# Weight sums in a two-layer attention and gated-MLP kernel, ordered behind the attention's last residual addition

## The chip, the cores and the metric

The kernel runs on one core of one Trainium2 chip. The metric is device time in microseconds (us), the median of several executions. The engines are named as the profile names them: PE does matmuls, DVE, ACT and POOL do elementwise work, SP issues most of the DMAs. ACT issues some as well. Each engine takes its own instructions in a fixed order, and semaphores hold an instruction until what it needs is done.

## The reference

Two layers, applied twice with the same weights, on x of 2048 tokens by 1024 features:

```python
x = x + A(layernorm(x))     # attention without softmax, 32 heads of 32
x = x + B(layernorm(x))     # gated MLP, 3584 hidden features
x = x + A(layernorm(x))
x = x + B(layernorm(x))
# A: q, k, v = x @ wqkv; phi(t) = where(t > 0, t + 1, exp(t)) + 1e-6
#    kv = phi(k)^T v; z = sum of phi(k); o = phi(q) kv / (phi(q) z + 1e-6); return o @ wo
# B: h = relu(x @ W_gate) * (x @ W_up); return h @ W_down
```

## The kernel before

Tokens come in 16 tiles of 128 (`x[t]`, resident in fp32). The four layers run one after the other: `layer_A(0)`, `layer_B(1)`, `layer_A(2)`, `layer_B(3)`.

**End of the attention.** `out_unit` makes one half (512 columns) of one token tile: eight matmuls (L557) into one PSUM bank, then the residual addition on DVE (L564) into `x[t]`. There are four such banks (tag "a"), so PE can run four units ahead of DVE. The first quarter of the tiles is done first, then quarters 1, 2 and 3. Beside them DVE and POOL still scale later quarters (L511 to L523), and the layer norm of the next layer already runs on finished tiles: statistics on DVE (L154, L159), `rstd` and the scaled tile `xnb` on ACT (L161, L162, L188), a transposing DMA issued on SP (L347) into `xnT`, and then the token sums `sums_x` on DVE (L712 to L715).

**The gated layer.** `layer_B` takes the tokens in two halves (`c`). Each 2x2 block product is done with seven products instead of eight (a Strassen-Winograd scheme), which needs sums of token blocks (`sums_x`) and sums of weight blocks. A unit `u` (`glu`, 14 per half) has two hidden tiles; for gate ("g") and up ("u") it makes seven products of four matmuls each (L739). Products 1, 2 and 3 read the raw weights, products 4 to 7 the sums. On the way DVE adds partial results (`zg`, `zu` at L770, `m5g`, `m5u` at L773), ACT copies and applies relu (L747, L756, L760), and DVE or POOL multiplies gate by up (L750, L777).

**The weight sums.** They are the same for all four passes over the weights, so they are formed once, during the first half of the first gated layer, and stored to DRAM; the later passes load them. `make_gu` forms the three sums of one gate or up weight tile on DVE, one instruction of 128x1024 elements (L677) and two of 128x512 (L679, L680), and stores them with a DMA on ACT's queue (L681). `make_d` loads two units' down weights into the tile `wd` (L690, on SP), forms four sums of 128x1024 elements (L694 to L697) and stores them (L698).

**What sets the order.** A list of later tasks (`_Later`) holds steps with a delay in ticks; a tick is one unit of the running stage, or one product of `glu`. The sums of unit 0 are entered at the start of the attention's last quarter with delay 1, those of unit u+1 at the start of unit u with delay 4, those of `make_d` with delay 4. The order of emission is only a priority: except inside `manual_schedule` blocks, a scheduler orders each engine's instructions by its own estimate of when their inputs are ready, and it may put a sum that is emitted late ahead of an addition that is emitted early. The weight loads go through a ring (`_Ring`) of slots in a pool of 16 buffers, issued on SP in program order; a load waits until its buffer's last reader is done and until an earlier DMA on the same semaphore has landed.

Of the kernel before, what the change touches and what calls it, by code (L numbers as in the profile page):

```python
# [8 lines left out]
ALU = mybir.AluOpType  # L9
# [80 lines left out]
class _Net:  # L90
# [313 lines left out]
    def layer_A(self, l, last_ln):  # L404
        nc, G, KT, D = self.nc, self.G, self.KT, self.D
        ring, later = self.ring, self.later
# [53 lines left out]
        def m_units(d):  # L460
            mt = self.temp([P, D], BF16, name=f"mt{l}_{d}")
            for h in range(H):
                ps = self.ps3.tile([P, NW], F32, tag="b")
                for t in range(self.ST):
                    nc.tensor.matmul(ps, lhsT=self.xn[l, t][:, d * P:(d + 1) * P],  # L465
                                     rhs=self.pk[l, t][:, h * NW:(h + 1) * NW],
                                     start=(t == 0), stop=(t == self.ST - 1))
                    if t == self.ST // 2 - 1:
                        later.tick()
                nc.scalar.activation(out=mt[:, h * NW:(h + 1) * NW], in_=ps, func=ACT.Copy)  # L470
                if h == H - 1:
                    later.at(2, lambda: kv_step(d, mt))
                later.tick()
# [30 lines left out]
        def z_chain(i):  # L504
            z_mult(*divmod(i, QT))
            if i < 10:
                later.at(2, lambda: z_chain(i + 1))

        def z_mult(sc, j):
            prod = ksum  # L510
            nc.gpsimd.tensor_tensor(out=prod, in0=pq_of[sc, j], in1=zrow, op=ALU.mult)  # L511
            later.at(2, lambda: z_sum(prod, sc, j))
# [17 lines left out]
        def fold_wo(n):  # L530

            n2, a = divmod(n, H)
            if n2 == 0:
                T.append(self.slot(f"T{l}_{a}", [P, 4, D]))
            ps = [pool.tile([P, NW], F32, tag=tag, name=f"fold{l}_{n}_{i}") for i, (pool, tag) in
                  enumerate(((self.kvp, "kv0"), (self.kvp, "kv1"), (self.ps3, "b"), (self.ps3, "b")))]
            wo = ring.get((l, f"o{n2}"))
            for b in range(R):
                g = a * R + b
                for i in range(R):  # L540
                    e = slice(i * HD, (i + 1) * HD)
                    nc.tensor.matmul(ps[i][b * HD:(b + 1) * HD, :], lhsT=kvT[e, g, e],
                                     rhs=wo[e, g, :], start=True, stop=True,
                                     tile_position=(i * HD, b * HD))
            for i in range(R):
                g = a * R + i
                dst = T[g // 4][:, g % 4, n2 * NW:(n2 + 1) * NW]
                if g % 2:
                    nc.scalar.activation(out=dst, in_=ps[i], func=ACT.Copy)
                else:  # L550
                    nc.vector.tensor_copy(out=dst, in_=ps[i])

        def out_unit(sc, j, n2):
            t = sc * QT + j
            ps = self.ps.tile([P, NW], F32, tag="a")
            for g in range(G):
                nc.tensor.matmul(ps, lhsT=pqT[sc][:, g, j * P:(j + 1) * P],  # L557
                                 rhs=T[g // 4][:, g % 4, n2 * NW:(n2 + 1) * NW],
                                 start=(g == 0), stop=(g == G - 1))
            cols = slice(n2 * NW, (n2 + 1) * NW)  # L560
            xs = self.x[t][:, cols]


            nc.vector.tensor_tensor(out=xs, in0=self.xb[t][:, cols] if l == 0 else xs,  # L564
                                    in1=ps, op=ALU.add)


        def column_major(f, q):
            return [lambda j=j, c=c: f(q, j, c) for c in range(H) for j in range(QT)]

        def row_major(f, q):
            return [lambda j=j, c=c: f(q, j, c) for j in range(QT) for c in range(H)]

        def run(*lists):

            n = max(len(u) for u in lists)
            for i in range(n):
                for u in lists:
                    if i < len(u):
                        u[i]()  # L580
                        later.tick()
# [26 lines left out]
        with self.tc.manual_schedule(engines={mybir.EngineType.DVE, mybir.EngineType.Pool}):  # L608
            ring.free_before((l, "v0"))
            later.at(5, z_row)  # L610
            later.at(7, lambda: z_chain(0))
            for d in range(KT):
                m_units(d)
            if l > 0:
                later.at(1, lambda: [self.bring_back(t) for t in range(self.NS)])
            q3 = row_major(q_unit, self.NQ - 1)
            out0 = column_major(out_unit, 0)

            def with_fold(u, i):
                return lambda: (u(), fold_wo(i // 2) if i % 2 == 0 else None)  # L620

            run(q3[:2])
            run([with_fold(u, i) for i, u in enumerate(q3[2:] + out0[:1])])
            run(out0[1:3])
            ring.free_slowly((l, "o0"), later, 2)
            for i in range(11, self.ST):
                later.at(1 + 3 * (i - 11), lambda i=i: z_mult(*divmod(i, QT)))
            run(out0[3:])
            for sc in range(1, self.NQ):
                if sc < 3:  # L630
                    self.ln_later(last_ln, sc - 1, 0, 3, 2)
                if sc == 2:
                    for j in range(QT):
                        later.at(3 * j + 6, lambda j=j: self.sums_x(last_ln, 0, j))
                if sc == 3 and l == 0:
                    for w in "gu":
                        later.at(1, lambda w=w: self.make_gu(ring.get((last_ln, 0, w, 0)), w, 0))
                run(row_major(out_unit, sc))


# [43 lines left out]
    def make_d(self, u):  # L684

        v = self.nc.vector
        t = self.slot(f"wd{u}", [P, 2, 4, NW])
        T = t[:, :, :, :].bitcast(F16)
        us = slice(u, u + 2)
        self.nc.sync.dma_start(out=t[:, :, :, :].rearrange("p u (h n) f -> p u h (n f)", h=2),  # L690
                               in_=self.wd_v[:, :, us, :].rearrange("p h u n -> p u h n"))

        def sums():
            v.tensor_tensor(out=T[:, :, 0, :], in0=t[:, :, 1, :], in1=t[:, :, 0, :], op=ALU.subtract)  # L694
            v.tensor_tensor(out=T[:, :, 1, :], in0=t[:, :, 3, :], in1=t[:, :, 1, :], op=ALU.subtract)
            v.tensor_tensor(out=T[:, :, 3, :], in0=t[:, :, 3, :], in1=T[:, :, 0, :], op=ALU.subtract)
            v.tensor_tensor(out=T[:, :, 2, :], in0=t[:, :, 2, :], in1=T[:, :, 3, :], op=ALU.subtract)  # L697
            self.later.at(1, lambda: self.nc.scalar.dma_start(  # L698
                out=self.td[:, us, :, :], in_=T))

        self.later.at(4, sums)

    def sums_x(self, l, c, j):

# [151 lines left out]

    def layer_B(self, l, final):
        ring = self.ring
        for c in range(2):
            hT = []  # L860
            first = l == 1 and c == 0
            for u in range(self.U):
                if u % 2 == 0:
                    hT.append(self.slot(f"h{l}_{c}_{u // 2}", dtype=F16))
                ring.load_to(ring.index((l, c, "g", u)) + 5)
                if first:
                    if u + 1 < self.U:
                        self.later.at(4, lambda u=u: [self.make_gu(ring.get((l, c, w, u + 1)), w, u + 1)
                                                      for w in "gu"])
                if first and u % 2 == 0:  # L870
                    self.make_d(u)
                self.glu(l, c, u, hT)
                if c == 0 and u == (self.U - 1 if first else 0):
                    after = self.last_put.ins
            if c == 0:
                self.ln_chunk(l, 1, 20, 3, 3, after)
            elif not final:
                self.ln_later(l + 1, 0, 28, 6, 4)
            self.down(l, c, hT, final)
# [68 lines left out]
```

## Time and profile before

| | us |
|---|---|
| median of 7 runs | 1500.2 |
| range of the 7 runs | 1498.98 to 1506.29 |
| the profiled execution | 1506.29 |
| its span in the trace | 1504.5 |
| PE busy | 1481.6 |
| DVE busy | 824.2 |
| ACT busy | 508.9 |
| POOL busy | 274.0 |

The profiled execution is the slowest of the seven. A line of the profile names an operation by its source line, the engine, and the tiles that it writes and reads; "ps<-T,pqT" is the attention's output product, "x<-x,ps" the residual addition, "w<-w" a sum of gate or up weights, "wd<-wd" a sum of down weights. Times are us from the start of the span unless marked ns. A bracket behind a row of the timeline is the time that its engine idled before it, and what ended that. The times of one stretch can be held against those of another that does the same work: the first and the second attention, or the two passes over the first token half.

### The profile page before, as it was taken

Reading aid. Unit: us, or ns where it says so; the run is one execution under the profiler, and the core shown is the slowest. Engines: PE = TensorE matmul, PEld = TensorE weight load, DVE = VectorE, ACT = ScalarE, POOL = GpSimd, SP = SyncE. Lnnn points to the kernel's source line nnn. Section 1 sums busy time; section 2 is a strip of 40 time slices with the busy share of each in tenths; the row PEclk is TensorE's granted clock in tenths of the full one; section 3 lists DMA queues with packets and bytes.
Section 4 is the critical chain, followed back from the end, with each engine's and each line's share of the span. In section 5 each row is a group of like instructions: output and inputs, shape, how many; then the busy total and the mean of one; then the engine's idle time right before and its main releaser. Section 6 shows DMA issues by size and latency. Waiting matters only on the chain.

```text
span 1504.5 us, 18590 instructions
## 1 busy us (share of the span) xinstructions
PE 1481.6 (98%) x7039; PEld 671.8 (45%) x7039; DVE 824.2 (55%) x1427; ACT 508.9 (34%) x911; POOL 274.0 (18%) x190
## 2 busy tenths in 40 slices
PE   9999998998899999999999999999999999999999
PEld 4444443443344444444444444444444444444444
DVE  8855588665585533447256645875335433444632
ACT  6751322333341243332047523233333203333300
POOL 1349340111000011110013474401111000111000
PEclk9999999999999999999999999999999999999999
DMA  9502449774568974435923027494344689444461
GB/s 276 102 29 49 113 79 292 252 228 171 185 199 204 318 242 139 140 129 169 269 42 71 29 43 227 90 285 140 113 150 137 195 239 293 140 140 140 147 210 42
DMA packets 313754, 242.92 MB, mean 161 GB/s; under 512 B 105280, under 2 KB 290880, under 8 KB 312768
## 3 DMA queue, kind: packets, MB, share of 16 engines
q1 hardware_dynamic: 302688, 214.07, 49.3%
q10 hardware_dynamic: 10976, 27.66, 4.9%
q8 instruction: 55, 0.90, 0.3%
q14 instruction: 35, 0.29, 0.1%
HBM read 186.65 MB, written 30.41 MB: 144 GB/s over the span
## 4 chain that ended last, share of the span: by engine, by line
PE 90%; DMA 4%; DVE 4%; issue 1%; ACT 0%; SPq 0%; DVEq 0%
PE ps L430 15%; PE dy L822 10%; PE yu L739 9%; PE yg L739 9%; PE ps L465 7%; PE dv L822 6%; PE dx L822 6%; PE xu L739 6%; PE xg L739 6%; PE zu L739 3%; PE zg L739 3%; PE vu L739 3%; PE vg L739 3%; PE ps L557 3%; DMA wd<-in_B_W_down_dram 3%; DVE x L564 1%
## 5 line engine op out<-in xcount | busy, mean ns | idle before, releaser
L739 PEld LDWEIGHTS <-w 128*128 128x128 f16 (+1 forms) x3136 | 307.3, 98 | 384.0 <-issue 15.2
L777 POOL TENSOR_TENSOR h<-m5u,m5g 128x512 f16<-128x512 f32 x56 | 72.0, 1286 | 832.9 <-DVE m5u L773 808.7
L430 PE MATMUL ps<-w,xnT 128*128 128x512 bf16 x1024 | 223.4, 379 | 0.2 <-ACT xnT L291 0.2
L822 PEld LDWEIGHTS <-h 128*128 128x128 f16 x1120 | 109.6, 98 | 132.2
L770 DVE TENSOR_TENSOR zg<-yg,m5g 128x512 f32<-128x512 f32 x56 | 39.1, 699 | 208.6 <-PE yg L739 204.4
L430 PEld LDWEIGHTS <-xnT 128*128 128x128 bf16 x1024 | 99.4, 98 | 119.9 <-issue 1.4
L739 PE MATMUL yu<-s,w 128*128 128x512 f16 x448 | 115.8, 381 | 6.9 <-DVE zu L770 6.8
L557 PE MATMUL ps<-T,pqT 128*128 128x512 bf16 x512 | 113.9, 385 | 6.6 <-DVE x L564 6.6
L739 PE MATMUL yg<-s,w 128*128 128x512 f16 x448 | 115.0, 379 | 3.3 <-DVE zg L770 3.3
L739 PE MATMUL xu<-xnT,w 128*128 128x512 f16 x448 | 115.1, 379 | 0.0
L739 PE MATMUL xg<-xnT,w 128*128 128x512 f16 x448 | 115.0, 379 | 0.0
L747 ACT ACTIVATE m5g<-m5g 128x512 f32<-128x512 f32 x56 | 35.2, 629 | 189.4 <-DVE m5g L773 183.9
L822 PE MATMUL dy<-w,h 128*128 128x512 f16 x448 | 98.0, 379 | 0.0
L822 PE MATMUL dx<-w,h 128*128 128x512 bf16 x448 | 97.3, 379 | 0.0
L511 POOL TENSOR_TENSOR kvc<-pq,kvc 128x1024 f32<-128x1024 bf16 x32 | 68.0, 2124 | 84.5 <-DVE den L516 71.1
L557 PEld LDWEIGHTS <-pqT 128*128 128x128 bf16 x512 | 50.5, 99 | 69.2 <-issue 10.9
L154 DVE BATCH_NORM_STATS2 stats<-x 128x6 f32<-128x512 f32 (+1 forms) x120 | 76.4, 672 | 0.5 <-DMA x<-in_A_x_dram 0.2
L161 ACT ACTIVATE rstd<-mv,eps 128x1 f32<-128x1 f32 x64 | 18.0, 289 | 156.0 <-DVE mv L159 155.8
L380 DVE SCALAR_TENSOR_TENSOR pq<-ps,e 128x512 bf16<-128x512 f32 x64 | 44.0, 687 | 48.5 <-ACT e L374 46.8
L516 DVE TENSOR_REDUCE den<-kvc 128x32 f32<-128x1024 f32 x32 | 38.9, 1215 | 54.1 <-POOL kvc L511 54.1
L447 POOL TENSOR_TENSOR kvc<-kvc,slab 128x512 f32<-128x512 f32 x46 | 53.9, 1179 | 78.2 <-DVE slab L380 60.9
L822 PEld LDWEIGHTS <-e 128*128 128x128 f16 x448 | 43.9, 98 | 52.8
(105 smaller groups left out, 1924.8 us busy)
## 6 DMA issues: line engine op xcount, KB each, us to landing
w<-in_B_W_gate_dram SPq DMA_DIRECT2D x56, 512.0 KB, 6.1
w<-in_B_W_up_dram SPq DMA_DIRECT2D x56, 512.0 KB, 4.6
w<-td SPq DMA_DIRECT2D x32, 896.0 KB, 4.7
w<-in_B_W_down_dram SPq DMA_DIRECT2D x24, 896.0 KB, 5.2
w<-tg SPq DMA_DIRECT2D x42, 512.0 KB, 6.9
w<-tu SPq DMA_DIRECT2D x42, 512.0 KB, 5.9
w<-in_A_wqkv_dram SPq DMA_DIRECT2D x10, 1024.0 KB, 8.5
tg<-w ACTq DMA_DIRECT2D x14, 512.0 KB, 5.2
```

The costliest lines, as they stand in the source:

```text
L154: self.nc.vector.bn_stats(out=stats[:, c, :], in_=src[:, c * fmax:(c + 1) * fmax])
L380: nc.vector.scalar_tensor_tensor(out=out, in0=ps, scalar=0.0, in1=e, op0=ALU.max, op1=ALU.add)
L430: nc.tensor.matmul(by_row(ps), lhsT=self.xnT[l, l_q][:, kt, j * P:(j + 1) * P], rhs=w[:, kt, :].rearrange("p (b i d) -> p i b d", i=R, d=H ...
L447: nc.gpsimd.tensor_tensor(out=ksum[:, cols], in0=ksum[:, cols], in1=pk, op=ALU.add)
L465: nc.tensor.matmul(ps, lhsT=self.xn[l, t][:, d * P:(d + 1) * P], rhs=self.pk[l, t][:, h * NW:(h + 1) * NW], start=(t == 0), stop=(t == sel ...
L511: nc.gpsimd.tensor_tensor(out=prod, in0=pq_of[sc, j], in1=zrow, op=ALU.mult)
L516: nc.vector.tensor_reduce(out=den, in_=heads(prod), axis=mybir.AxisListType.X, op=ALU.add)
L557: nc.tensor.matmul(ps, lhsT=pqT[sc][:, g, j * P:(j + 1) * P], rhs=T[g // 4][:, g % 4, n2 * NW:(n2 + 1) * NW], start=(g == 0), stop=(g == G ...
L739: nc.tensor.matmul(ps, lhsT=W[w][m][:, k, :], rhs=A[m][:, k, :], start=start and k == 0, stop=k == 3, skip_group_check=True)
L770: nc.vector.tensor_tensor(out=Z[w], in0=Y[w], in1=V[w], op=ALU.add)
L777: nc.gpsimd.tensor_tensor(out=h[:, 3, :], in0=V["u"], in1=V["g"], op=ALU.mult)
L822: nc.tensor.matmul(banks[j], lhsT=A(k)[:, j * P:(j + 1) * P], rhs=w[:, i, :], start=start and k == 0, stop=k == self.U - 1, skip_group_che ...
```

## The change

The attention's last residual addition is kept in `self.last_x` (each `out_unit` overwrites it, so that it is the last one traced). The sums of units 1 to 13 and those of the down weights are traced inside `issue_after(self.last_x.ins)`, which makes every instruction of the block on that addition's engine, DVE, stand behind it in DVE's order. The sums of unit 0 get no such edge, but they are entered with delay 8 instead of 1, at the end of the last quarter. The stores on ACT's queue and the loads on SP's get no edge. In `layer_B` a helper `behind` does this. The second gated layer has no sums and is not touched.

```diff
@@ out_unit
-            nc.vector.tensor_tensor(out=xs, in0=self.xb[t][:, cols] if l == 0 else xs,
-                                    in1=ps, op=ALU.add)
+            self.last_x = nc.vector.tensor_tensor(out=xs, in0=self.xb[t][:, cols] if l == 0 else xs,
+                                                  in1=ps, op=ALU.add)
@@ layer_A
                 if sc == 3 and l == 0:
                     for w in "gu":
-                        later.at(1, lambda w=w: self.make_gu(ring.get((last_ln, 0, w, 0)), w, 0))
+                        later.at(8, lambda w=w: self.make_gu(ring.get((last_ln, 0, w, 0)), w, 0))
@@ make_d
+        def behind(fn):
+            with self.tc.issue_after(self.last_x.ins):
+                fn()
...
-        self.later.at(4, sums)
+        self.later.at(4, lambda: behind(sums))
@@ layer_B
+        def behind(it, fn):
+            with self.tc.issue_after(it.ins):
+                fn()
...
-                        self.later.at(4, lambda u=u: [self.make_gu(ring.get((l, c, w, u + 1)), w, u + 1)
-                                                      for w in "gu"])
+                        self.later.at(4, lambda u=u: behind(self.last_x, lambda: [
+                            self.make_gu(ring.get((l, c, w, u + 1)), w, u + 1) for w in "gu"]))
```

In the order that the scheduler makes of it, DVE's last addition is followed by the sums of gate 0 and gate 1, mixed, then up 0, up 1, the down weights of units 0 and 1, and gate 2. PE's order changes in the first five units of the gated layer: it begins with eight matmuls that read raw weights (`xg`, `xu`), and products of the next unit stand between those of the current one. From the sixth unit on the order on all engines is the one before.

## The prediction

> **What bounds the kernel now.** I read the busy shares first, then busy time by stretch, then the timeline and the chain of waits around the one stretch that the change touches.
>
> ```profile
> PE 1481.6 (98%) x7039; PEld 671.8 (45%) x7039; DVE 824.2 (55%) x1427; ACT 508.9 (34%) x911; POOL 274.0 (18%) x190
> PE ps L557 <- DVE x L564: 6.6, 2, 5.6
> ```
>
> The first line is the page's: the matmuls bound the kernel, so only time in which PE idles or runs at a lower clock can be won, some 23 us of idling in all. The second line, from the list of waits, says who PE waited for most while it did the attention's output product: the residual addition (L564), twice, 5.6 us the longer time. The stretches show where that is (columns: length, PE, PEld, DVE, ACT and POOL busy, granted PE clock, DMA share, GB/s):
>
> ```profile
> 181.40:244.24 62.84, 56.20 (x248) 24.74 (x249) 53.86 (x113) 14.78 (x26) 17.89 (x9) 0.95 0.57 140
> 244.24:427.18 182.94, 172.70 (x786) 77.29 (x785) 115.57 (x199) 65.65 (x112) 18.00 (x14) 0.98 0.67 219
> 938.87:993.20 54.33, 53.63 (x249) 24.11 (x248) 45.16 (x94) 14.77 (x26) 17.91 (x9) 1.00 0.62 140
> 993.20:1162.60 169.40, 169.38 (x785) 76.83 (x786) 81.39 (x134) 66.89 (x120) 17.70 (x14) 1.00 0.49 157
> ```
>
> Rows 1 and 3 are the same work, the output product of the first and of the second attention. The first takes 8.5 us more. Rows 2 and 4 are the 14 units of the gated layer's first token half, first and second time: 13.5 us more. The weight sums (L677 to L680, L694 to L697) are formed on DVE only around the first, so both losses are theirs. The change touches the first loss at its root; the second comes later and is a different wait. The timeline of the first (start, length, engine; the brackets name the idle time before):
>
> ```profile
> 225.73 5.34 PE L557 MATMUL ps<-T,pqT 128*128 128x512 bf16 x24 [1.06 <-DVE x L564]
> 230.64 0.69 DVE L677 TENSOR_TENSOR w<-w 128x1024 f16<-128x1024 bf16 x1
> 231.25 0.42 DVE L680 TENSOR_TENSOR w<-w 128x512 f16<-128x512 bf16 x1
> 231.58 0.42 DVE L679 TENSOR_TENSOR w<-w 128x512 f16<-128x512 bf16 x1
> ...
> 234.03 0.69 DVE L694 TENSOR_TENSOR wd<-wd 128x1024 f16<-128x1024 bf16 x1 [0.49 <-DMA wd<-in_B_W_down_dram]
> ...
> 235.91 0.68 DVE L564 TENSOR_TENSOR x<-x,ps 128x512 f32<-128x512 bf16 x1
> 236.65 7.76 PE L557 MATMUL ps<-T,pqT 128*128 128x512 bf16 x24 [5.58 <-DVE x L564]
> ```
>
> From 230.64 to 235.91 DVE does nothing but weight sums, ten of them, and waits 0.49 us for a load. Behind them stands the addition of tile 12's second half, which frees the PSUM bank of PE's next unit. PE stops at 231.07 and goes on at 236.65. Its next 24 matmuls take 7.76 us, where 24 of the batch before took 5.34: the clock was at half.
>
> **The change, part by part.** The sum is made on the profiled execution: 1506.29 us, span 1504.5 and 1.8 around it, the slowest of the seven. The median of the runs shown is 1500.2, 6.1 less; I carry a difference in us over to the median.
>
> 1. Removed: the stall. In the changed program every sum that stood among the additions comes after the last one (tile 15, second half). Tile 12's addition then follows the second group of token sums (L712 to L715). Without the sums between them these end at about 230.0 to 230.6, and a bank is free again before 231.07. That removes 5.58 us of idling and 7.76 - 24 x 0.218 = 2.5 us of half clock (0.218 = 13.93/64, from the chain's row of 64 matmuls of L557): 8.1 us.
>
> 2. The clock's part of it. The trace drops the clock when PE has stood for some us:
>
> ```profile
> 234.00:235.00 1.00, 0.00 (x0) 0.00 (x0) 0.96 (x3) 0.00 (x0) 0.00 (x0) 0.87 1.05 430
> 235.00:241.00 6.00, 4.35 (x11) 1.55 (x11) 6.00 (x15) 1.24 (x1) 0.00 (x0) 0.50 0.64 207
> 340.00:341.00 1.00, 0.00 (x0) 0.00 (x0) 0.52 (x1) 0.00 (x0) 0.00 (x0) 0.78 0.56 225
> ```
>
> Clock 0.87 over 234 to 235 means half clock from 234.74, 3.7 us into the 5.58 us gap; 0.78 over 340 to 341 means 340.56, 2.5 us into the other long gap (338.1 to 343.0). The 1.06 us gap cost none: the slice after it stays at 1.00. So I count the 2.5 us as certain in every run. [...]
>
> 3. Not removed: the 1.06 us gap at 225.73. DVE waits there for a transposed tile (L712), whose chain starts at an addition released by PE at 195.33; the three sums that leave the stretch before 195 shorten nothing on it. Bounds 0 and 1.06 of gain; I take 0.
>
> 4. Added: the first unit's sums now stand between the last addition and the first matmuls that read them. PE's last output matmul would end at 231.07 + 5.2 = 236.3. The second attention has no sums and shows when the last addition can start: PE's output ends at 992.5, and these two rows follow:
>
> ```profile
> 993.22 1.04 PE L739 MATMUL vg<-s,w 128*128 128x512 f16 x4 [0.71 <-DVE s L712]
> 994.21 0.68 DVE L564 TENSOR_TENSOR x<-x,ps 128x512 f32<-128x512 f32 x1
> ```
>
> So 1.7 us after PE's end: here 238.0. Behind it DVE starts something every 0.61 us for a 128x1024 sum and every 0.33 us for a 128x512 one (the starts 230.64, 231.25, 231.58 above). The order in the changed program is gate 0, gate 1 (L677 each), L679 of both, L680 of gate 0, L677 of up 0, L680 of gate 1, L679 of up 0, three of up 1, L680 of up 0, and then down-weight sums between the products' own additions. Gate 0's first sum is ready at 239.2, up 0's at 241.5. PE begins with eight matmuls that need no sum (xg, xu: 1.7 us, to 238.05). vg then waits until 239.3: 1.25 us. vu, nine groups of DVE work later, comes at 241.6 after vg, xg and half of yg: 0.1. Then zg (L770) stands behind two down-weight sums, whose load was issued at 228.44 and landed by 234.03, and ends at 245.6; PE is back for it at 245.5: 0.2 with the signal. zu stands behind two more and gate 2's L677 and is ready at 248.7, PE at 248.75: 0.1. Together 1.7 us of new gaps, none as long as the 2.5 us after which the clock fell.
>
> Bounds: at best the 0.71 us of the second attention's vg; at worst, if the last transposed tile lands later, vg waits 2.8, the rest stays at 0.4, and the clock falls: half from 340.56 to about 347.4 (0.81 over 347 to 348 in the same view) is 6.8 us, at most 3.4 lost. That is 6.6.
>
> 5. What is queued behind the moved sums. ACT issues the stores of the sums (L681, L698) in its own order, so its copies for PE (L756, L760) wait behind them. Store of gate 0 goes at 240.9, of up 0 at 243.1; the copy of vu follows at 243.2 and zu needs it at 248: covered by 4 us. SP reissues a slot or a semaphore only after these stores landed: gate 4's load goes when gate 0's store is down, 240.9 + 5.2 (median of the stores) = 246, down pair 2's at about 247, where before they went at 244.67 and 246.37 in a program that was 6 us behind. They land at 252 and 254 with 5.5 and 7.0 us (medians of that stretch); DVE comes to them at about 256 and 258.5. Covered by 4 us; if the cover were gone, PE would wait the excess at zg or zu of unit 1. Fewer stores before 240 also leave the loads of unit 2 and 3 free to go earlier. From the sixth unit on, the order on PE, DVE, ACT and SP is the old one, and the waits there (13.5 us) start at a PE event that frees a slot, followed by a load and a sum. They move with PE, neither won nor lost.
>
> Sum: 8.1 - 1.7 = 6.4 us. Forecast 1500.2 - 6.4 = 1493.8.
>
> **The rivals.** *The gain stays small.* The first unit's wait reaches the clock, or a load of units 1 to 4 comes late once: 8.1 - 6.6 = 1.5 us at the least, time 1497 to 1498.7. For it: the last transposed tile shares the DMA engines with up 2 and gate 3, issued at the same time; against: the second attention issues more loads there and its tile still landed after 4.7 us.
>
> *Slower: the late stores starve the ring of weights.* The loads of gate 4 and down pair 2 are tied to stores that come 6 to 10 us later against PE, and down pair 4's load to pair 2's store. One row shows what a crowded stretch does:
>
> ```profile
> 329.29 11.16 DMA wd<-in_B_W_down_dram
> ```
>
> If store and load both took 11 us, gate 4's would land at 263, 7 us after DVE wants it, and zg of unit 1 stands behind it; with half clock that is 9 to 10 us lost against 6.4 won: 1503 to 1504. It decides once a load of units 1 to 4 comes more than about 4 us late plus the drop. Against it: the other four loads of that kind on the chain took 5.6 to 8.6 us, and the stretch 240 to 300 shows no wait of PE.
>
> *The stall is the profiled execution's own.* It is 6.1 us above the median, close to the stall. Then the median has nothing to win, 1500. Against: nine tenths of that stall is DVE at work in a fixed order, only 0.49 us of it a wait for a transfer; the 11.16 us load with its 4.92 us gap and half clock is the better candidate for the 6.1. That the change does not do what it says is excluded: the sums do stand behind.
>
> **How the numbers follow.** Forecast case (new gaps of 0.7 to 4 us, gains of 4 to 8.5): 0.74. Small gain 0.13, stall only in the profiled run 0.06, slower 0.07. A measurement can tell 0.2%, 3 us, from no change. Faster by more: the forecast case, and about two thirds of the small gains, 0.83. Within: the rest of these and most of the third rival, 0.10. Slower 0.07. Range: below, 8.1 - 0.7 + 1.06 = 8.5 us, and the fastest run lies 1.2 us under its median: 1490.5. Above, the small gain's end of 1.5 us with half a us of spread: 1499.2.
>
> **What would show it.** Right: no sum among the additions, no PE gap over 1 us between 227 and 236 and clock 1.00 there, vg waiting 1 to 1.5 us for the sum of L677, the first unit starting near 236.3, and the stretch of 14 units at 182 to 185 us. Wrong: half clock after the first unit's wait, gaps for loads in units 1 to 4, or a 14-unit stretch longer by what the first stretch wins.

## The result and the profile after

The changed kernel has a median of 1492.68 us over 16 runs (1490.5 to 1498.51), against 1500.2 before (41 runs by now, with the same median as the first seven): 7.5 us less, a ratio of 0.9951 [0.994, 0.9962]. The forecast was 1493.8.

The profiled execution took 1497.82 us with a span of 1496.0, 8.5 us less than the profiled one before. The page's busy shares and three rows of PE's list of waits (us in total, times, longest):

```profile
PE 1479.4 (99%) x7039; PEld 670.9 (45%) x7039; DVE 825.5 (55%) x1427; ACT 508.3 (34%) x911; POOL 274.8 (18%) x190
...
PE yu L743 <- DVE zu L774: 6.4, 4, 5.2
PE yg L743 <- DVE zg L774: 1.7, 3, 0.8
PE ps L557 <- DVE x L564: 0.9, 1, 0.9
```

No engine does less work; PE's busy time falls by 2.2 us mostly because the 24 matmuls that ran at half clock now run at the full one. The wait of the output product (L557) on the residual addition went from 6.6 us in two waits to 0.9 in one. The busy times by stretch (length, PE, PEld, DVE, ACT, POOL, granted clock, DMA share, GB/s), in the four stretches of the prediction:

```profile
182.14:236.75 54.61, 53.70 (x264) 24.25 (x249) 45.71 (x95) 14.78 (x26) 17.89 (x9) 1.00 0.51 107
236.75:418.69 181.94, 173.44 (x786) 77.04 (x785) 124.45 (x218) 64.86 (x112) 18.80 (x14) 0.98 0.71 236
930.47:984.77 54.30, 53.71 (x264) 24.18 (x248) 45.25 (x95) 14.77 (x26) 17.90 (x9) 1.00 0.62 143
984.77:1154.00 169.23, 169.22 (x785) 76.73 (x785) 81.33 (x134) 66.90 (x120) 17.54 (x14) 1.00 0.50 158
```

The first attention's output product takes 54.6 us instead of 62.8, at full clock, and stands within 0.3 us of the second attention's: the first loss is gone nearly whole. The 14 units take 181.9 instead of 182.9. The product begins 0.7 us later, from a delay far ahead of the change, so -8.2 - 1.0 + 0.7 = -8.5, the difference of the spans. Times of this trace are to be read 0.7 us earlier when they are held against those of before. The second loss, 181.9 against 169.2, is still there.

The timeline of the place (start, length, engine; in brackets the idle time before):

```profile
226.39 10.52 PE L557 MATMUL ps<-T,pqT 128*128 128x512 bf16 x48 [0.91 <-DVE x L564]
230.50 0.68 DVE L564 TENSOR_TENSOR x<-x,ps 128x512 f32<-128x512 bf16 x1
232.61 1.25 SPq L347 DMA_TRANSPOSE xnT<-xnb  x1
236.07 0.42 DVE L716 TENSOR_TENSOR s<-xnT 128x512 f16<-128x512 f16 x1
236.75 1.03 PE L743 MATMUL xg<-xnT,w 128*128 128x512 f16 x4
237.53 0.68 DVE L564 TENSOR_TENSOR x<-x,ps 128x512 f32<-128x512 bf16 x1
238.13 1.29 DVE L677 TENSOR_TENSOR w<-w 128x1024 f16<-128x1024 bf16 x2
238.87 1.04 PE L743 MATMUL vg<-s,w 128*128 128x512 f16 x4 [0.23 <-DVE w L677]
```

Where two batches of 24 matmuls stood with 5.58 us between them, 48 run as one. Tile 12's addition starts at 230.50 instead of 235.91. The last transposing DMA is issued at 232.61 (238.02 before), its token sums begin at 236.07, the last addition at 237.53, and only then the weight sums. `vg` waits 0.23 us for its first one.

### The profile page after: what moved, and what is told of

The parts are those of the page before. It is cut to its first block, busy times and chain, and to the rows that moved or that the text cites. A ratio compares the mean times of both kernels' runs of the same rounds, so it can differ in the third digit from the quotient of the medians.

```text
span 1496.0 us, 18583 instructions
## 1 busy us (share of the span) xinstructions
PE 1479.4 (99%) x7039; PEld 670.9 (45%) x7039; DVE 825.5 (55%) x1427; ACT 508.3 (34%) x911; POOL 274.8 (18%) x190
## 4 chain that ended last, share of the span: by engine, by line
PE 89%; DVE 5%; DMA 4%; issue 1%; ACT 0%; SPq 0%; DVEq 0%
PE ps L430 15%; PE dy L826 10%; PE yu L743 9%; PE yg L743 9%; PE ps L465 7%; PE dx L826 6%; PE dv L826 6%; PE xg L743 6%; PE xu L743 6%; PE zu L743 3%; PE zg L743 3%; PE vu L743 3%; PE vg L743 3%; PE ps L557 2%; DMA wd<-in_B_W_down_dram 2%; DVE x L564 1%
## 5 line engine op out<-in xcount | busy, mean ns | idle before, releaser
L743 PEld LDWEIGHTS <-w 128*128 128x128 f16 (+1 forms) x3136 | 307.1, 98 | 383.2 <-issue 14.3
L743 PE MATMUL yu<-s,w 128*128 128x512 f16 x448 | 115.8, 381 | 6.4 <-DVE zu L774 6.4
L743 PE MATMUL yg<-s,w 128*128 128x512 f16 x448 | 115.3, 379 | 1.8 <-DVE zg L774 1.7
L743 PE MATMUL xu<-xnT,w 128*128 128x512 f16 x448 | 115.0, 379 | 0.1
L743 PE MATMUL xg<-xnT,w 128*128 128x512 f16 x448 | 115.0, 379 | 0.0
L557 PE MATMUL ps<-T,pqT 128*128 128x512 bf16 x512 | 111.3, 379 | 0.9 <-DVE x L564 0.9
L557 PEld LDWEIGHTS <-pqT 128*128 128x128 bf16 x512 | 49.9, 98 | 61.5 <-issue 1.6
```

Source lines behind the costliest of these rows:

```text
L743: nc.tensor.matmul(ps, lhsT=W[w][m][:, k, :], rhs=A[m][:, k, :], start=start and k == 0, stop=k == 3, skip_group_check=True)
```

## The experiments

The theory: each microsecond of DVE work ahead of tile 12's addition, beyond what PE's free banks cover, stands in PE's path; the change takes that work away. Rivals: the granted clock, not DVE, is what costs; the sums of the down weights and their load are what costs; the new delay does it alone, without the edges. The helper puts lines behind it four higher than before (L739 is L743), and added code shifts them further. Ratios are to the kernel before, run on the same chip.

**The changed kernel again**, beside other kernels on two more chips.

> The changed kernel as it is, once more, beside the next two. 7 to 8 us faster than before; the output product's stretch 8 us shorter; clock 1.00 there.

> The changed kernel a third time, to hold the next against it on one chip: 1492.7 to 1493.2.

Measured: 1493.2 us, 0.9943 [0.9928, 0.9959], and 1493.86 us, 0.996 [0.9946, 0.9975]. The output product takes 54.8 and 54.6 us, so the gain of the first stretch is in all three executions that were profiled. The medians of before beside them are 1499.55 and 1499.56 us: 6.4 and 5.7 us less here, where the first comparison gave 7.5. The 14 units vary: 176.5 and 178.1 us, where the profiled execution above had 181.9. What differs most is one load, the fifth of the down weights. From the chain and the timeline of the first profile after, the load, the sum that waits for it, and PE behind that sum:

```profile
323.35 11.41 DMA wd<-in_B_W_down_dram
334.78 0.69 DVE L698 TENSOR_TENSOR wd<-wd 128x1024 f16<-128x1024 bf16 x1 [5.47 <-DMA wd<-in_B_W_down_dram]
337.33 1.86 PE L743 MATMUL yu<-s,w 128*128 128x512 f16 x4 [5.17 <-DVE zu L774]
```

And the same two instructions in the first repeat:

```profile
330.24 0.69 DVE L698 TENSOR_TENSOR wd<-wd 128x1024 f16<-128x1024 bf16 x1 [1.83 <-DMA wd<-in_B_W_down_dram]
332.79 1.02 PE L743 MATMUL yu<-s,w 128*128 128x512 f16 x4 [1.53 <-DVE zu L774]
```

The gap of 5.17 us also drops the clock (four matmuls in 1.86 us instead of 1.02). The first profile's execution is 6.3 us slower than this one (1491.53), and its 14 units are 5.4 us longer. This load, not the removed stall, makes most of the difference between these two executions; that it also makes the spread of the other runs is likely, but not shown.

**Edges without the later delay** (on the changed kernel).

```diff
-                        later.at(8, lambda w=w: self.make_gu(ring.get((last_ln, 0, w, 0)), w, 0))
+                        later.at(1, lambda w=w: self.make_gu(ring.get((last_ln, 0, w, 0)), w, 0))
```

> The changed kernel with its edges, but unit 0's sums entered with delay 1 as before. In DVE's order the six sums of unit 0 (two of 0.61 us, four of 0.33 us, 2.5 us) then stand ahead of tile 12's second addition; all other sums stay behind the last one. Theory (PE stops because sums stand ahead of that addition): the addition starts at about 233.0 instead of 230.5, PE idles about 2 us before tile 14's second half, too short for the clock to fall, and vg then waits for nothing: 1.5 to 2 us slower than the changed kernel, so 5.5 us faster than before, about 1494.5. Rival (the gain comes from the new order in the gated layer's first units): as the changed kernel, 1492.7. Rival (it is unit 0's delay that brings the gain): as before, 1500.

Measured: 1496.29 us, 0.9972 [0.9955, 0.9989], a gain of 4.2 where 5.5 was expected. The six sums of unit 0 (229.95 to 233.00) now stand ahead of tile 12's addition, 3.05 us of DVE, and the timeline of PE shows:

```profile
233.73 5.34 PE L557 MATMUL ps<-T,pqT 128*128 128x512 bf16 x23 [2.55 <-DVE x L564]
```

The gap is 0.5 us shorter than the sums. The clock stays at 1.00, and the product takes 57.5 us, 2.9 more than in the changed kernel.

**The later delay without edges** (on the kernel before, the same line with 8 for 1).

> The kernel before with only unit 0's delay changed from 1 to 8; no edges. In DVE's order two sums of up 1 (0.95 us) stand ahead of tile 12's second addition, and single sums of up 1 and of the down weights between the later ones, the first down sum behind a load that landed at 234.0. Theory: tile 12's addition starts near 231.5, PE idles about 0.5 us, the later additions have slack, and 1 us at most is lost at the first unit: 6 to 7 us faster than before, 1493 to 1494, though none of the edges is there. Rival (the edges bring the gain): no faster than before by more than 1 us, 1499 to 1500.

Measured: 1497.36 us, 0.9989 [0.9972, 1.0007]; the expected gain of 6 to 7 is missing (the medians differ by 3.1 us, the ratio by 1.6, and the interval reaches from 4.2 to -1.0). The first half of the expectation came true: of the gate and up sums only two are left ahead of tile 12's addition, the gap there is 0.64 us, and PE begins the gated layer at 236.77, as in the changed kernel. The tail went wrong. Without edges the scheduler spreads the down-weight sums between the later additions, and one of them waits for its load:

```profile
231.59 5.34 PE L557 MATMUL ps<-T,pqT 128*128 128x512 bf16 x23 [0.64 <-DVE x L564]
233.87 0.69 DVE L694 TENSOR_TENSOR wd<-wd 128x1024 f16<-128x1024 bf16 x1 [0.34 <-DMA wd<-in_B_W_down_dram]
240.42 0.68 DVE L564 TENSOR_TENSOR x<-x,ps 128x512 f32<-128x512 bf16 x1
241.02 1.29 DVE L677 TENSOR_TENSOR w<-w 128x1024 f16<-128x1024 bf16 x2
241.76 1.89 PE L739 MATMUL vg<-s,w 128*128 128x512 f16 x4 [3.10 <-DVE w L677]
```

The last addition slips from 237.53 to 240.42, unit 0's sum with it, `vg` waits 3.10 us and the clock drops (1.89 us for four). So each part clears its own end, the delay the head of the stretch and the edges its tail. That both together win more than the two gains added up is not shown: the intervals are too wide for that.

**Edges on the down-weight sums alone** (on the kernel before).

```diff
-        self.later.at(4, sums)
+        self.later.at(4, lambda: behind(sums))
```

> The kernel before with one part of the change: only the down-weight sums get the edge behind the last addition. DVE's order then has twelve sums of gates and ups between tile 7's statistics and tile 12's second addition, 5.4 us, and no wait for the down load. Theory (it is DVE's time ahead of that addition, whoever's sums fill it): the gap of PE stays at about 5 us, no faster than before by more than 1 us, 1499.5 to 1500.5. Rival (the wait for the down load in front of the addition is what costs): 5 us faster or more.

Measured: 1498.5 us, 0.9992 [0.9977, 1.0007]. The wait of 0.49 us for the down weights is gone, but the gate and up sums still stand there, and PE waits 4.34:

```profile
235.66 1.44 PE L557 MATMUL ps<-T,pqT 128*128 128x512 bf16 x3 [4.34 <-DVE x L564]
```

The rival that blames the down weights' load falls. The profiled execution was the fastest of the twelve (1494.95 us), and the stall stands in it all the same.

**DVE work put back into the changed kernel.** Nine or five statistics instructions on a finished tile, whose results nobody reads, ahead of tile 12's second addition.

```diff
+            if l == 0 and (sc, j, n2) == (3, 0, 1):
+                for i in range(9):      # 5 in the second kernel
+                    pad = self.small.tile([P, nc.vector.BN_STATS_DIM], F32, tag="pad")
+                    nc.vector.bn_stats(out=pad, in_=self.x[0][:, 0:NW])
```

> The changed kernel with nine statistics instructions (L154's kind, 0.6 us each, 5.4 us; nobody reads them) on DVE just ahead of tile 12's second addition, in the place that the weight sums had. Theory: tile 12's addition moves from 230.5 to 235.9, PE idles 4.5 to 5.5 us and the clock falls: 7 to 8 us slower than the changed kernel, 1500, though every weight sum stands behind the last addition. Rival (what counts is where the weight sums, their stores and loads stand, not DVE's time ahead of the addition): less than 2 us slower, 1493 to 1494.5.

> The changed kernel with five statistics instructions (3.0 us, nobody reads them) ahead of tile 12's second addition, where e5_dose_9 had nine (5.4 us). Theory (each us on DVE ahead of that addition beyond a slack of about 0.5 us is a us of PE): PE idles 2.3 to 2.7 us, the clock stays, the output product's stretch is 2.5 to 3 us longer than the changed kernel's 54.6, and the time 2.5 to 3 us longer, 1495.5 to 1496. Rival (what counts is the fall of the clock): the cost comes at once with the fall, and this dose costs under 1 us or about 7.

Measured: 1500.19 us, 1.0 [0.9984, 1.0015], with nine; 1496.72 us, 0.9979 [0.9965, 0.9993], with five, 2.9 above the changed kernel beside it. The row of PE with nine, then with five:

```profile
236.19 1.44 PE L557 MATMUL ps<-T,pqT 128*128 128x512 bf16 x3 [4.84 <-DVE x L568]
```

```profile
233.57 5.34 PE L557 MATMUL ps<-T,pqT 128*128 128x512 bf16 x23 [2.47 <-DVE x L568]
```

Work that touches no weights, with no load and no store, brings the whole loss back: 5.35 us of it leave a gap of 4.84 and nothing of the gain. This shows the cause. With five the clock stays at 1.00, and yet the output product takes 57.3 us, 2.7 more than in the changed kernel; so the rival that the granted clock is what costs falls as well. The price can be read across the kernels. In the changed one tile 12's second addition starts 4.06 us after the pair of additions before it (226.44 to 230.50). How much longer that takes in the others, in us, against PE's gap there:

| kernel | addition later by | PE's gap |
|---|---|---|
| delay without edges | 1.13 | 0.64 |
| five statistics | 2.98 | 2.47 |
| edges without delay | 3.05 | 2.55 |
| edges on the down sums | 4.84 | 4.34 |
| nine statistics | 5.35 | 4.84 |
| before | 6.07 | 5.58 |

The gap is the lateness less 0.5 us in every row, whatever the work was: 0.5 us is the slack that the four banks leave here, and beyond it DVE's time is PE's, one for one.

**The clock kept up through the stall** (on the kernel before): 22 matmuls into a spare bank, ahead of the unit that waits.

```diff
+            if l == 0 and (sc, j, n2) == (3, 2, 1):
+                warm = self.ps3.tile([P, NW], F32, tag="b", name="warm")
+                for g in range(22):
+                    with self.tc.issue_after(self.last_mm.ins):
+                        self.last_mm = nc.tensor.matmul(warm, lhsT=pqT[sc][:, g % G, 0:P],
+                                                        rhs=T[0][:, g % 4, 0:NW], start=True, stop=True)
```

> The kernel before, with 22 matmuls more on PE whose result nobody reads, queued just ahead of tile 14's second half, in the place of the 5.6 us gap; 22 x 0.218 = 4.8 us. DVE's order is that of before. The gap stays, but the clock should not fall. Theory with the clock term of 2.5 us counted in every run: 2.5 us faster than before, 1497.7, clock 1.00 from 230 to 245, and the 24 matmuls behind take 5.3 us. [...] If the clock had no part: 0, or 0.5 slower where the dummies outlast the gap.

Measured: 1500.15 us, 0.9998 [0.9983, 1.0014]: no gain is shown, though the interval still holds the 2.5 us. The clock did what it should: 1.00 from 230 to 250, and the waiting unit's 24 matmuls took 5.34 us, not 7.76. Yet up to the first gated matmul the stage came out only 0.6 us shorter than before (62.3 against 62.9). The timeline shows where the rest of the 2.4 us went:

```profile
232.04 0.69 DVE L686 TENSOR_TENSOR w<-w 128x1024 f16<-128x1024 bf16 x1 [0.79 <-DMA w<-in_B_W_up_dram]
233.90 4.91 PE L559 MATMUL warm<-T,pqT 128*128 128x512 bf16 x21
240.00 5.34 PE L565 MATMUL ps<-T,pqT 128*128 128x512 bf16 x24 [1.19 <-DVE x L573]
241.38 1.24 SPq L347 DMA_TRANSPOSE xnT<-xnb  x1
246.20 0.42 DVE L721 TENSOR_TENSOR s<-xnT 128x512 f16<-128x512 f16 x1
246.67 0.59 PE L748 MATMUL vg<-s,w 128*128 128x512 f16 x2 [1.32 <-DVE s L721]
```

Some 0.4 us went to tile 12's addition, which came later than before because a sum ahead of it waited 0.79 us for an up weight. And PE, done sooner, waited 1.32 us at `vg` for the last token sums. The transposed tile that they read was not late: DVE came to it at 246.20, 4.82 us after its issue, without a wait, behind additions and weight sums. But the added matmuls had also changed PE's order. Here the gated layer begins with `vg`, which needs those sums; in the kernel before it begins with six matmuls, 1.3 us, that do not:

```profile
244.24 1.03 PE L739 MATMUL xg<-xnT,w 128*128 128x512 f16 x4
245.11 0.59 PE L739 MATMUL xu<-xnT,w 128*128 128x512 f16 x2
245.54 1.03 PE L739 MATMUL vg<-s,w 128*128 128x512 f16 x4
```

So this run does not settle what the half clock alone is worth in the order of before.

**Later down-weight sums** (on the changed kernel), against the second loss: the edge of `make_d` hangs on the last product put into `h` instead of the last addition, with a delay of 9 or 15 ticks.

```diff
-            with self.tc.issue_after(self.last_x.ins):
+            with self.tc.issue_after(self.last_put.ins):
...
-        self.later.at(4, lambda: behind(sums))
+        self.later.at(9, lambda: behind(sums))      # 15 in the second kernel
```

> The changed kernel, with the down-weight sums entered at delay 9 instead of 4 and ordered behind the last product-of-gate-and-up (L750's kind) of that moment instead of the last residual addition. In DVE's order they move by one unit, some 12 us, behind the load that they wait for. In the changed kernel's profile DVE waits 11.6 us for down loads in the 14-unit stretch, and PE's longest gap there (5.2 us, with half clock behind it) starts with one. Theory (the rest of the 13 us loss in that stretch is DVE waiting in order for down loads): 5 to 8 us faster than the changed kernel, 1485 to 1488. Rival (the loads are bound by slots, which the later sums free later, so the wait moves to the gate loads): within 2 us of the changed kernel, or slower.

> As the one before, with delay 15, so that the sums come behind the unit's last product, among the sums of the next unit. Theory: as the one before, 5 to 8 us faster than the changed kernel; the slot of the down tile is held some us longer. Rival: the slot is freed so late that a later load waits for it and PE for that: no faster than the changed kernel.

> The variant with the down-weight sums behind the unit's last product, once more: 2 us faster than the changed kernel, 1491, with a spread under 2 us, if the first comparison holds; within 1 us of it if that was chance.

Measured with 9: 1500.19 us, 0.9992 [0.9978, 1.0006]; the gain expected is missing and the whole gain of the change with it. The lists of waits, one row of PE, one of ACT and one of DVE (the latter two of the gated layer's first half):

```profile
PE xu L743 <- ACT yu L764: 10.7, 4, 2.8
ACT yu L764 <- DVE h L754: 18.1, 5, 4.3
DVE w L677 <- DMA w<-in_B_W_up_dram: 6.6, 1, 6.6
```

DVE no longer waits for the down weights, but in one place 6.6 us for an up weight and in one 4.5 us for a gate weight, much as the rival had it. The product `h` is late, ACT's copy `yu` waits for it, and PE, ready for `xu`, loses 10.7 us in four gaps. The chain from `h` to PE is the profile's; how much of each `h`'s delay comes from the load and how much from the sums moved beside it was not separated.

Measured with 15: 1491.05 us, 0.9932 [0.9917, 0.9947], beside 1493.2 for the changed kernel, and again on another chip 1491.46, 0.9947 [0.9932, 0.9962], beside 1493.86. The 14 units are steady at 175.7 and 175.9 us, with no wait for down weights:

```profile
235.72:411.41 175.69, 171.54 (x785) 76.34 (x784) 125.16 (x216) 64.27 (x112) 17.29 (x14) 1.00 0.72 245
DVE w L677 <- DMA w<-in_B_W_up_dram: 4.7, 3, 2.8
```

It was 2.2 to 2.4 us below the changed kernel in both places and never above 1492.5, but the two intervals against before overlap: faster than before is shown, faster than the changed kernel likely, by some 0.15%. Of the 5 to 8 us expected only these came. The 11.6 us of DVE's waits for down weights are gone, and those for up weights are 4.7 us where they were 3.6. The expectation was reckoned from the first profile after, whose 14 units are 4 to 5 us longer than those of the repeats; against that execution the 14 units are indeed 6 us shorter.

## Why the prediction was right

**The stall (step 1)** was the right place, at the right size. Tile 12's addition was predicted to follow the token sums that end at 230.0 to 230.6; it came at 230.50 (229.8 in the times of before), and PE ran on without a gap. The returned dose shows DVE work as the cause, and the total removed, 8.2 us of the output product's stretch, is the 8.1 of the sum.

**The clock (step 2).** The 2.5 us of half clock were there in this execution and are gone, and the stretch is shorter by the idling and them together. Counting them "as certain in every run" was right for the fall and too strong for its size. In the two kernels with a gap of 4.84 and 4.34 us the clock fell too (0.66 over 235 to 240 in both), but from the first matmul behind the gap to the first gated one PE took 6.8 and 6.5 us, where it was 7.6 before and 5.3 at full clock: 1.5 and 1.2 us lost instead of 2.3. What the half clock is worth when it alone is taken away stays open: 0.3 us by the times, with an interval from -2.1 to 2.6, in a run that changed PE's order as well. The rows show that these 24 matmuls took 2.4 us longer (7.76 against 5.34 us); that the kernel pays that price in full, no run here confirms. The sum came out right because the change moves DVE's whole chain, the additions as well as the last transposing DMA (238.02 to 232.61, 6.1 us after allowing for the later start), so that little else was late at the end of the stretch.

**The gap that stays (step 3)** stayed: 0.91 us at 226.39, where it had been 1.06.

**The new gaps (step 4)** were over-sized. The path was as told: last addition, L677, `vg`. The predicted wait of 1.25 us, given as a sign of being right, was 0.23, and unit 1's `zg` cost 0.26, where 0.2 was expected for unit 0's. The term that was wrong is the start of the last addition, taken as 1.7 us after PE's output ends, as in the second attention. It was 0.6 (236.91 to 237.53). In the second attention DVE waits for the last transposed tile, which lands 4.7 us after its issue; here it landed after 3.1 us, and DVE came to it without a wait, 3.46 us after its issue (232.61 to 236.07). All of step 4 measured some 0.5 us, not 1.7. With it the sum gives 8.1 - 0.5 = 7.6. That the medians show 7.5 is closer than they can tell: the repeats gave 6.4 and 5.7 us by their medians, 8.5 and 6.0 by their ratios.

**The late stores (step 5)** were covered, as said. The loads of gate 4 and of the second pair of down weights were issued here:

```profile
243.18 0.37 SPq L667 DMA_DIRECT2D w<-in_B_W_gate_dram  x1
244.43 0.52 SPq L690 DMA_DIRECT2D wd<-in_B_W_down_dram  x1
```

That is some 3 us before the times predicted, and no gap of PE over 0.3 us stands in units 0 to 4. The 14-unit stretch, predicted at 182 to 185 us, was 181.9 here and 176.5 and 178.1 in the repeats. The prediction took one execution's stretch for the kernel's.

**The rivals.** That late stores starve the ring: no load of the first units came late. That the stall was the profiled execution's own: the median gained 7.5 us, the dose brings the loss back in the median too, and the profiles of the kernels that keep the sums there show the stall again. What the prediction offered instead for that execution's 6.1 us excess, the 11 us load with its gap and half clock, fits: the first profile after has it too (11.41 us), and the first repeat, 6.3 us faster, has not (7.77).

## What to carry to other kernels

Look at what stands in an in-order engine's queue ahead of the instruction that frees a buffer of the bounding engine: here, past the 0.5 us that the free buffers covered, each microsecond there cost one (gaps of 0.64 to 5.58 us), with DVE's busy share at 55%. Order the work behind the last such instruction and also enter it late; by the ratios the edges alone gave 4.2 us and the delay alone 1.6 (not told from nothing) of the 7.4. A half-clock stretch is not yet a gain of its own (with the clock kept at 1.00 the time fell by 0.3 us, with an interval from -2.1 to 2.6): look at what else is late at its end, and whether the experiment on it keeps the order of the engines.

## What the runs showed of the hardware

**The clock fell after some gaps of 2.5 us and not after others.** In the gated layer PE stood for 2.52 us with only the edges, and for 2.57 us with the 9-tick delay; both times the clock fell, in the second after PE was back at work. Gaps of 2.55 us (edges only) and 2.47 us (five statistics) in the output product left it at 1.00, and so did one of 2.70 us (to 334.60) later in the 9-tick kernel and two more behind it, of 5.4 us together. The two falls, by stretch, in the one kernel and in the other (columns as above):

```profile
335.00:336.00 1.00, 0.22 (x1) 0.10 (x1) 1.00 (x3) 0.00 (x0) 0.00 (x0) 0.78 0.68 279
336.00:337.00 1.00, 1.00 (x3) 0.29 (x2) 0.96 (x3) 0.63 (x1) 0.00 (x0) 0.50 0.26 90
```

```profile
305.88 1.34 PE L743 MATMUL xu<-xnT,w 128*128 128x512 f16 x4 [2.57 <-ACT yu L764]
306.00:307.00 1.00, 1.00 (x4) 0.34 (x3) 1.00 (x3) 0.33 (x1) 0.00 (x0) 0.73 0.94 377
```

By the clock shares, PE had stood for 2.3 us when the clock fell in the one (335.56), and had been back for 0.6 us in the other (306.46). In the kernel before it had stood for 3.7 us (234.74) and for 2.5 us (340.56). Nor was the half clock always of one length: it lasted 6.83 us both times there (to 241.57 and 347.38) and in the first profile after (335.26 to 342.08), and 3.4 us in the two kernels here. What decides whether a gap of 2.5 us costs, and for how long, these runs do not show.

**From issue to use is not the time of the transfer.** From the issue of the last transposing DMA to the token sums it took 3.46 us in the changed kernel, 4.8 in the kernel with the added matmuls (241.38 to 246.20) and 5.3 before (238.02 to 243.32). By the trace the tile landed 3.1 us after its issue in the changed kernel and before, and in none of the three did DVE wait for it; the rest is DVE, which had additions and sums ahead of it. In the second attention (before) it landed later, after 4.7 us, and there DVE waited for it:

```profile
992.73 0.42 DVE L712 TENSOR_TENSOR s<-xnT 128x512 f16<-128x512 f16 x1 [1.23 <-DMA xnT<-xnb]
```

That value, which the prediction took over from another layer, is the largest single error in its sum.
